# Loading a weight as two blocks of 8 partitions and one of 112 instead of one of 128

## The chip, the cores and the metric

The kernel runs on one core of a Trainium2 chip. The time is device microseconds of one execution. All numbers below are of undisturbed ("fast") runs. The span that the profile shows (187.6 us before) is about 1.3 us shorter than the timed figure of the same execution (188.87 us).

Weights and caches come from HBM into SBUF over 16 DMA engines. In the trace of the kernel before, the load of `w_gate` is 128 packets of 15360 B, one for each partition row, and 16 completions. From 20 to 180 us 16 packets are in flight for 90% of the time, and 15, 17 or 18 nearly all the rest, so each engine works at one packet after the other.

## The reference, cut to what matters

One decoding step of a transformer layer for two tokens: modulation, attention over a cache, then a gated feed-forward layer. The change touches only the load of `w_gate`, at the end:

```
h = layernorm(x) * (1 + cb) + sb                      # x: 2 x 640
x = x + gb * ((gelu(h @ w_gate) * (h @ w_up)) @ w_down)   # w_gate, w_up: 640 x 1536, w_down: 1536 x 640
```

Nearly all the work is reading: 76.88 MB in bf16.

## The kernel before

All loads go from one queue (SP), in the order in which they are needed: modulation weights, query weights, 16 K and 16 V blocks, three blocks of the output weight `wo`, then `w_gate`, two blocks of `w_up`, four of `w_down`. Every one of these loads fills all 128 partitions; blocks are cut by columns. The last loads, and the matmuls that wait for them:

```python
# each partition p holds rows 5p..5p+4 of w_gate: 5 x 1536 x 2 B = 15360 B, one packet
S.dma("sp", k_dma(wg_v.rearrange("p k n -> p (k n)"),
                  B_w_gate.rearrange("(p k) n -> p (k n)", k=KT)), sem_wg,
      writes=["wg"], deps=r3_dead, name="ld_wg")
# ... (w_up in WU_SPLIT = [(0,3),(3,2)], packets of 9216 and 6144 B;
#      w_down in WD_SPLIT = [(9,3),(0,5),(5,3),(8,1)], packets of 3840, 6400, 3840, 1280 B)
ffn_gu(0, wg_v, "gate", [(0, KT, "wg")])               # 20 matmuls, wait for ln2 and wg
# ... gelu
ffn_gu(1, wu_v, "up", [(k0, nk, ("wu", ci)) for ci, (k0, nk) in enumerate(WU_SPLIT)])
# ... geglu, transpose, then w_down block by block, two DVE operations, the store
```

Of the kernel before, what the change touches and what calls it, by code (L numbers as in the profile page):

```python
# [119 lines left out]
def bass_adaLN_cond__sliding_block_cached__geglu_ffn__decode_kernel(  # L120
# [20 lines left out]
    KT = D // P  # L141
# [28 lines left out]
    WQ_SPLIT = [(0, 2), (2, 3)]  # L170
    WO_SPLIT = [(0, 28), (28, 17), (45, 3)]
    NWQ, NWO = len(WQ_SPLIT), len(WO_SPLIT)
    WU_SPLIT = [(0, 3), (3, 2)]
    WD_SPLIT = [(9, 3), (0, 5), (5, 3), (8, 1)]
    RB = 16
# [11 lines left out]
    with es:  # L187
        S = _Sched(nc, es)
# [6 lines left out]
        wg_v = r3[:, 0:KT * F].rearrange("p (k n) -> p k n", k=KT)  # L195
        wu_v = r3[:, KT * F:2 * KT * F].rearrange("p (k n) -> p k n", k=KT)
# [56 lines left out]
        def bank(k):  # L253
            return ("bank", k)
# [1 line left out]
        sem_x = S.sem("d_x")  # L256
        sem_c = S.sem("d_c")
        sem_wm = S.sem("d_wm")
        sem_wg = S.sem("d_wg")
        sem_wu = [S.sem("d_wu%d" % i) for i in range(len(WU_SPLIT))]  # L260
        sem_wd = [S.sem("d_wd%d" % i) for i in range(len(WD_SPLIT))]
        sem_ring = [S.sem("d_ring%d" % i) for i in range(NS)]
# [2 lines left out]
        def k_dma(dst, src):  # L265
            return lambda e: e.dma_start(dst, src)  # L266
# [40 lines left out]
        def declare_ring(consumed=()):  # L307
            ring_state["done"].update(consumed)
            while ring_state["next"] < len(items):
                it = items[ring_state["next"]]  # L310
                if not all(h in ring_state["done"] for h in before_of[it]):
# [7 lines left out]
                       writes=["wm"], name="ld_wm")  # L319
# [4 lines left out]
        for nm, t in (("scT", scT), ("oT", oT), ("aT", aT)):  # L324
# [6 lines left out]
             reads=["ones_f"], writes=["ident_f"], name="ident_f")  # L331
        S.op("pool", lambda e: e.tensor_copy(out=ident_b[:, :], in_=ident_f[:, :]),
             reads=["ident_f"], writes=["ident_b"], name="ident_b")
# [3 lines left out]
             reads=["ones_b"], writes=["selrow"], name="selrow")  # L337
# [3 lines left out]
             reads=["ones_b"], writes=["selg"], name="selg")  # L341
        for b in range(B):
# [4 lines left out]
                 reads=["ones_b"], writes=[("selq", b)], name="selq%d" % b)  # L347
# [4 lines left out]
             reads=["ones_b"], writes=["ztmp"], name="ztmp")  # L352
# [6 lines left out]
             reads=["ones_f", "bcL"], writes=["bcL"], name="bcLh")  # L359
# [5 lines left out]
             reads=["bcR"], writes=["bcR"] + [("bcR", z) for z in range(2)], name="bcRd")  # L365
# [4 lines left out]
             reads=["ident_f"], writes=["mask_h"], name="mask_h")  # L370
        S.op("dve", lambda e: e.tensor_reduce(out=st32[:, :], in_=ident_f[:, :].rearrange("p (i m) -> p m i", m=32), axis=AX.X, op=ALU.add),
             reads=["ident_f"], writes=["st32"], name="st32")
# [3 lines left out]
             reads=["st32"], writes=["selstat"], name="selstat")  # L376
# [3 lines left out]
        def c_T(e):  # L380
            last = None
            for j in range(KT):
# [4 lines left out]
             reads=[bank(BK_T)], writes=["scT"], name="silu")  # L387
        S.op("dve", lambda e: e.tensor_copy(out=X[:, :], in_=xr[:, :]),
             reads=["xr"], writes=["X"], name="x_f32")
# [20 lines left out]
        def ln_mod(tag, opc_idx, s_idx, dst_bf):  # L410
# [7 lines left out]
            def f(e):  # L418
# [14 lines left out]
             reads=["mask_h"], writes=["maskc"], name="maskc")  # L433
        S.op("dve", lambda e: e.tensor_reduce(out=zsel[:, :, X0:X0 + P].rearrange("p q (h m) -> p q h m", m=32)[:, :, :, 0],
                                              in_=ztmp[:, :, :, :].rearrange("p i q h -> p q h i"), axis=AX.X, op=ALU.max),
             reads=["ztmp", "zsel"], writes=["zsel"], name="zsel")

        mod_pe = []
        for half in range(2):
            def f(e, half=half):  # L440
                last = None
                for k in range(KT):
# [9 lines left out]
                 reads=[bank(half)], writes=[("modR", half)], name="mod%d_evac" % half)  # L452
            S.op("dve", lambda e, half=half: e.tensor_scalar(out=opc[:, half, :], in0=modR[:, 3 * half + 1, :], scalar1=1.0, scalar2=None, op0=ALU.add),
                 reads=[("modR", half)], writes=[("opc", half)], name="opc%d" % half)
# [17 lines left out]
        for n in range(NQB):  # L472
            if n % 2 == 0:
                S.op("act", lambda e, n=n: e.activation(out=qrow[:, n * QW:(n + 1) * QW], in_=ps[:, n, :], func=ACTF.Copy),  # L474
                     reads=[bank(n)], writes=[("qrow", n)], name="q1_evac%d" % n)
            else:
                S.op("dve", lambda e, n=n: e.tensor_copy(out=qrow[:, n * QW:(n + 1) * QW], in_=ps[:, n, :]),  # L477
                     reads=[bank(n)], writes=[("qrow", n)], name="q1_evac%d" % n)
        for u, (n, b) in enumerate((n, b) for n in range(NQB) for b in range(B)):
            bk = BK_T + u % 4  # L480
            S.op("pe", lambda e, n=n, b=b, bk=bk: e.matmul(ps[:, bk, :], lhsT=selq[:, b, :], rhs=qrow[:, n * QW:(n + 1) * QW], start=True, stop=True),
                 reads=[("selq", b), ("qrow", n)], writes=[bank(bk)], name="q2_%d_%d" % (n, b))
            S.op("act", lambda e, n=n, b=b, bk=bk: e.activation(out=qbc[:, b, n * QW:(n + 1) * QW], in_=ps[:, bk, :], func=ACTF.Copy),  # L483
                 reads=[bank(bk)], writes=[("qbc", b, n)], name="q2_evac%d_%d" % (n, b))
# [98 lines left out]
        for g in range(NG + 2):  # L583
# [23 lines left out]
            if prev:  # L607
# [5 lines left out]
             reads=[bank(BK_OT)], writes=["oT"], name="oT")  # L613
        for ci, (t0, n) in enumerate(WO_SPLIT):
            def f(e, ci=ci, t0=t0, n=n):
# [11 lines left out]
        assert ring_state["next"] == len(items)  # L627

        r3_dead = [wm_dma] + mod_pe
        S.dma("sp", k_dma(wg_v.rearrange("p k n -> p (k n)"), B_w_gate.rearrange("(p k) n -> p (k n)", k=KT)), sem_wg,  # L630
              writes=["wg"], deps=r3_dead, name="ld_wg")
        for ci, (k0, nk) in enumerate(WU_SPLIT):
            S.dma("sp", k_dma(wu_v[:, k0:k0 + nk, :].rearrange("p k n -> p (k n)"), B_w_up.rearrange("(p k) n -> p (k n)", k=KT)[:, k0 * F:(k0 + nk) * F]), sem_wu[ci],
                  writes=[("wu", ci)], deps=r3_dead, name="ld_wu%d" % ci)
        wd_src = B_w_down.rearrange("(p r) n -> p (r n)", r=FC)
        for ci, (r0, nr) in enumerate(WD_SPLIT):
# [5 lines left out]
             reads=[bank(BK_M), ("modR", 0)], writes=["lnt"], name="ga_attn")  # L642
        S.op("dve", lambda e: e.tensor_tensor(out=X[:, :], in0=lnt[:, :], in1=X[:, :], op=ALU.add),
             reads=["lnt", "X"], writes=["X"], name="x1")
# [3 lines left out]
        def ffn_gu(bk, wv, name, splits):  # L648
            for ci, (k0, nk, key) in enumerate(splits):
                def f(e, k0=k0, nk=nk):  # L650
                    last = None
                    for k in range(k0, k0 + nk):
                        wk = wv[:, k, :].rearrange("p (m i r) -> p i m r", i=NR, r=FR)
                        for i in range(NR):
                            last = e.matmul(ps[32 * i:32 * i + B, bk, 0:FT].rearrange("p (m r) -> p m r", r=FR), lhsT=h2T[:, k, :],
                                            rhs=wk[:, i, :, :], start=(k == 0), stop=(k == KT - 1), tile_position=(0, 32 * i))
                    return last
                S.op("pe", f, reads=["ln2_out", key], writes=[bank(bk)], name="ffn_%s%d" % (name, ci))

        ffn_gu(0, wg_v, "gate", [(0, KT, "wg")])  # L660
        S.op("act", lambda e: e.activation(out=gl[:, :], in_=ps[:, 0, 0:FT], func=ACTF.Gelu_apprx_tanh),
             reads=[bank(0)], writes=["gl"], name="gelu")
        ffn_gu(1, wu_v, "up", [(k0, nk, ("wu", ci)) for ci, (k0, nk) in enumerate(WU_SPLIT)])
        S.op("dve", lambda e: e.tensor_tensor(out=aR[:, :], in0=ps[:, 1, 0:FT], in1=gl[:, :], op=ALU.mult),
             reads=[bank(1), "gl"], writes=["aR"], name="geglu")

        def a_T(e):
            last = None
            for i in range(NR):
# [7 lines left out]
             reads=[bank(2)], writes=["aT"], name="aT")  # L677
        for ci, (r0, nr) in enumerate(WD_SPLIT):
            def f(e, r0=r0, nr=nr):
# [10 lines left out]
             reads=[bank(BK_OT), ("modR", 1)], writes=["fin"], name="gb_y")  # L690
        S.op("dve", lambda e: e.tensor_tensor(out=finb[:, :], in0=fin[:, :], in1=X[:, :], op=ALU.add),
             reads=["fin", "X"], writes=["finb"], name="outR")
        S.dma("sp", k_dma(out[:, 0, :].rearrange("b (i n) -> i b n", i=NR), finb[0:P:RB, :]),
              sem_out, reads=["finb"], name="st_out")
# [35 lines left out]
```

## Time and profile before

| | before |
|---|---|
| time, median of 4 runs beside the change | 189.06 us (188.81 to 189.14) |
| HBM read | 76.88 MB, 410 GB/s over the span |
| load queue, share of 16 engines' span | 97.1% |
| `w_gate`: last completion | 175.37 us |
| `w_down`: last completion | 184.75 us |

These are lines of the page of the kernel before. The rows `DMA` and `GB/s` cut the span in 40 slices (a digit is tenths of busy DMA engines). The queue rows give packets, MB and the share of 16 engines' span. The last line is the chain that ended last.

```profile
span 187.6 us, 2409 instructions
...
DMA  7999998999999999999999999999999999999991
GB/s 254 402 451 435 430 459 372 422 435 424 430 422 422 427 425 426 427 424 420 419 432 432 422 423 422 421 438 422 424 423 422 419 488 428 416 384 442 398 396 45
...
q1 hardware_dynamic: 6492, 76.88, 97.1%
q8 instruction: 8, 0.13, 0.3%
...
DMA 71%; DVE 15%; PE 7%; ACT 2%; SPq 2%; issue 1%
```

DMA is full from the third slice on at about 425 GB/s. The chain of waits in order of time ends with this kernel's last load (start us, length us, what):

```profile
152.72 31.64 DMA r<-in_B_w_down_dram
184.41 0.72 PE ps L684 x16
185.16 0.34 DVE fin L689
185.52 0.32 DVE finb L691
```

The `w_down` loads were all issued long before; the last two blocks landed at 184.37 and 184.75 us (completion records), and after that come only the last matmuls, two DVE operations and the store. So the span of this kernel is the landing of its last load plus 3 us. The issue list (KB each, us from issue to landing) shows `w_gate` as one load:

```profile
r<-in_B_w_gate_dram SPq DMA_DIRECT2D x1, 1920.0 KB, 25.0
```

These are PE's matmuls on `w_gate`, on the first block of `w_up`, and on the last blocks of `w_down` (start us, busy us, ..., in brackets the idle time before and what ended it), from the timeline of the kernel before:

```profile
175.51 1.89 PE L655 MATMUL ps<-r,h2T 128*2 128x384 bf16 x20 [0.28 <-DVE h2T L427]
178.19 1.21 PE L655 MATMUL ps<-r,h2T 128*2 128x384 bf16 x12 [0.79 <-DMA r<-in_B_w_up_dram]
...
184.41 0.70 PE L684 MATMUL ps<-r,aT 128*17 128x160 bf16 x16 [0.62 <-DMA r<-in_B_w_down_dram]
```

The gate matmuls waited for the layer norm (DVE), not for `w_gate`, which had landed at 175.37. The later ones waited for DMA. And here is DMA in three stretches of 5 us, shortly before and while `w_gate` and `w_up` come in (last three columns: granted clock, DMA busy share, GB/s):

```profile
165.00:170.00 5.00, 2.40 (x88) 2.07 (x80) 0.00 (x0) 0.00 (x0) 0.00 (x0) 0.74 0.95 392
170.00:175.00 5.00, 1.69 (x86) 1.39 (x78) 2.33 (x9) 2.98 (x5) 0.00 (x0) 0.95 0.99 415
175.00:180.00 5.00, 3.34 (x52) 1.05 (x48) 0.17 (x1) 0.71 (x2) 0.00 (x0) 0.71 1.00 412
```

The trace holds each DMA packet with its start and duration, and each completion. Here a 15360 B packet takes 578 ns (median of 128; 573 to 591) and a 12288 B packet 464 ns (median): none of the 128 was visibly held up by another. But the engines do not stand level. The 16 completions of `w_gate` came at these times after the first of them:

```
0  0.04  0.05  0.08  0.15  0.16  0.28  0.52  0.81  0.98  1.53  1.55  1.61  1.67  1.69  1.92 us
```

The kernel ends with the latest engine. Part of the spread has a cause in this trace: the 8 packets of 16384 B of the instruction queue took 0.93 to 1.10 us each, between two packets of the load queue, and the data packet after one of them took 938 instead of 460 ns. By these figures (1.10 + 0.94 - 0.46) an engine falls about 1.6 us behind, an estimate; the same sum gives 1.5 to 1.6 us for each of the seven that began before 174 us. Six completions above are at least 1.53 us late; of the last `w_down` load, seven are over 1.4 us late.

### The profile page before, as it was taken

The page shows a single profiled execution, that of the slowest core. Times are in us where ns is not written, and L with a number is a line of the kernel's source. Part 1 is how long each engine was busy: PE and PEld are TensorE (multiplying, and loading weights), DVE is VectorE, ACT ScalarE, POOL GpSimd, SP SyncE. Part 2 cuts the span into 40 slices and gives each one's busy share as a digit, 9 for nine tenths or more (in the row PEclk, how much of TensorE's full clock was granted, in tenths as well). Part 3 has the DMA queues.
Part 4 walks back from the last instruction along what each step waited for, and adds up shares of the span by engine and source line. Part 5 has one row for each costly group of instructions (what it writes and reads, how often), then busy time and mean ns, then how long its engine had stood idle before and what let it go on. Part 6 is the DMA issues. An engine that isn't in the chain of part 4 may idle for free.

```text
span 187.6 us, 2409 instructions
## 1 busy us (share of the span) xinstructions
PE 107.5 (57%) x1039; PEld 51.1 (27%) x1039; DVE 98.2 (52%) x147; ACT 29.9 (16%) x72; POOL 5.1 (3%) x23
## 2 busy tenths in 40 slices
PE   0014730742968887676676655675497395364462
PEld 0011200210323443333423323233253152353121
DVE  6131100019588988886595695775865933003211
ACT  3041100082001221112011110210120103103400
POOL 8200000000000000000000000000000000000000
PEclk9999999997587999999879999999969967569696
DMA  7999998999999999999999999999999999999991
GB/s 254 402 451 435 430 459 372 422 435 424 430 422 422 427 425 426 427 424 420 419 432 432 422 423 422 421 438 422 424 423 422 419 488 428 416 384 442 398 396 45
DMA packets 6518, 77.03 MB, mean 411 GB/s; under 512 B 746, under 2 KB 876, under 8 KB 1516
## 3 DMA queue, kind: packets, MB, share of 16 engines
q1 hardware_dynamic: 6492, 76.88, 97.1%
q8 instruction: 8, 0.13, 0.3%
q10 hardware_dynamic: 16, 0.01, 0.0%
q14 instruction: 2, 0.02, 0.0%
HBM read 76.88 MB, written 0.00 MB: 410 GB/s over the span
## 4 chain that ended last, share of the span: by engine, by line
DMA 71%; DVE 15%; PE 7%; ACT 2%; SPq 2%; issue 1%
DMA ring<-in_A_k_cache_dram 37%; DMA ring<-in_A_wq_dram 17%; DMA r<-in_B_w_down_dram 17%; DVE prod L490 9%; PE ps L502 4%; DVE S_sb L509 4%; PE ps L467 2%; SPq L266 2%; ACT qbc L483 2%; DVE ps L485 1%; DVE M L512 1%; ACT qrow L474 1%; PE ps L526 0%; DVE bcR L519 0%; PE ps L684 0%
## 5 line engine op out<-in xcount | busy, mean ns | idle before, releaser
L490 DVE TENSOR_TENSOR prod<-ring,qbc 128x3072 bf16<-128x3072 bf16 x32 | 55.9, 1751 | 14.3 <-DMA ring<-in_A_k_cache_dram 14.3
L502 PE MATMUL ps<-prod,ident_b 128*128 128x512 bf16 x192 | 52.9, 419 | 14.4 <-DVE prod L490 14.4
L502 PEld LDWEIGHTS ps<-prod,ident_b 128*128 128x128 bf16 x192 | 17.5, 104 | 40.2 <-DVE prod L490 17.5
L509 DVE TENSOR_REDUCE S_sb<-ps 128x32 f32<-128x1024 f32 x16 | 19.3, 1206 | 2.1 <-PE ps L502 2.1
L526 PE MATMUL ps<-bcR,bcL 5*128 5x4 f32 x32 | 6.1, 258 | 21.9 <-DVE bcR L519 21.9
L563 ACT ACTIVATE On<-ps,rden 128x384 bf16<-128x384 f32 x16 | 9.3, 580 | 43.5 <-DVE rden L561 21.1
L551 PE MATMUL ps<-ring,E_sb 128*8 128x384 bf16 x256 | 15.5, 369 | 0.0
L534 ACT ACTIVATE E_sb<-Sb_sb 128x128 bf16<-128x128 f32 x16 | 5.0, 310 | 56.4 <-DVE Sb_sb L531 56.4
L467 PE MATMUL ps<-ring,hT 128*2 128x512 bf16 x60 | 6.7, 626 | 9.8 <-DMA ring<-in_A_wq_dram 8.8
L526 PEld LDWEIGHTS ps<-bcR,bcL 5*128 5x128 f32 x32 | 4.7, 183 | 26.1 <-DVE bcR L519 26.1
L477 DVE CAST qrow<-ps 128x512 bf16<-128x512 f32 x1 | 0.7, 692 | 15.7 <-PE ps L467 15.7
L622 PE MATMUL ps<-ring,oT 128*17 128x160 bf16 x192 | 5.5, 294 | 5.6 <-DMA ring<-in_A_wo_dram 5.6
L531 DVE TENSOR_TENSOR Sb_sb<-S_sb,ps 128x128 f32<-128x128 f32 x16 | 4.6, 287 | 7.6 <-PE ps L526 7.6
L540 PEld LDWEIGHTS ps<-denp,maskc 128*128 128x128 f32 x32 | 7.1, 224 | 3.7 <-ACT E_sb L534 0.9
L641 DVE TENSOR_TENSOR lnt<-ps,modR 128x160 f32<-128x160 f32 x1 | 0.3, 325 | 12.6 <-PE ps L622 12.6
L445 PE MATMUL ps<-r,scT 128*17 128x480 bf16 x40 | 4.3, 597 | 3.9 <-DMA r<-in_w_mod_dram 3.9
L622 PEld LDWEIGHTS ps<-ring,oT 128*17 128x17 bf16 x192 | 4.9, 117 | 6.2 <-DMA ring<-in_A_wo_dram 6.2
L551 PEld LDWEIGHTS ps<-ring,E_sb 128*8 128x8 bf16 x256 | 5.1, 90 | 3.7 <-issue 1.2
L396 PE MATMUL ps<-st,selstat 128*128 128x2 f32 x4 | 0.9, 298 | 8.6 <-ACT sqj L392 8.6
L467 PEld LDWEIGHTS ps<-ring,hT 128*2 128x2 bf16 x60 | 1.7, 114 | 14.7 <-DMA ring<-in_A_wq_dram 9.7
L576 PE MATMUL ps<-On,zsel 128*128 128x96 bf16 x64 | 5.2, 241 | 0.7 <-ACT On L563 0.7
L540 PE MATMUL ps<-denp,maskc 128*128 128x1 f32 x32 | 5.1, 230 | 0.8 <-ACT E_sb L534 0.8
(81 smaller groups left out, 71.2 us busy)
## 6 DMA issues: line engine op xcount, KB each, us to landing
ring<-in_A_k_cache_dram SPq DMA_DIRECT2D x16, 1536.0 KB, 24.4
ring<-in_A_v_cache_dram SPq DMA_DIRECT2D x16, 1536.0 KB, 24.2
r<-in_w_mod_dram SPq DMA_DIRECT2D x1, 4800.0 KB, 14.3
ring<-in_A_wq_dram SPq DMA_DIRECT2D x1, 4608.0 KB, 32.3
ring<-in_A_wo_dram SPq DMA_DIRECT2D x1, 4480.0 KB, 23.4
ring<-in_A_wq_dram SPq DMA_DIRECT2D x1, 3072.0 KB, 21.2
ring<-in_A_wo_dram SPq DMA_DIRECT2D x1, 2720.0 KB, 24.1
r<-in_B_w_gate_dram SPq DMA_DIRECT2D x1, 1920.0 KB, 25.0
```

Source lines behind the costliest of these rows:

```text
L467: last = e.matmul(ps[32 * i:32 * i + B, n, :], lhsT=hT[:, k, :], rhs=wv[:, kk, i, n * QW:(n + 1) * QW], start=(k == 0), stop=(k == KT - 1) ...
L490: S.op("dve", lambda e: e.tensor_tensor(out=prod[:, 2 * (g % 2) + ci, :, :], in0=ring[:, sl, ci * JC * Dh:(ci + 1) * JC * Dh].rearrange("p ...
L502: last = e.matmul(o_ap, lhsT=ident_b[:, :], rhs=prod[:, pz, :, t * GC:(t + 1) * GC], start=(t == 0), stop=(t == NCH - 1))
L509: S.op("dve", lambda e: e.tensor_reduce(out=S_sb[:, z, :], in_=ps[:, 2 * z:2 * z + 2, :].rearrange("p k (j c) -> p (k j) c", c=GC), axis=A ...
L526: S.op("pe", lambda e: e.matmul(ps[:, BK_T, P:P + HQ], lhsT=bcL[:, :], rhs=bcR[:, z, :], start=True, stop=True), reads=[("bcR", z), "bcL"] ...
L531: S.op("dve", lambda e: e.tensor_tensor(out=Sb_sb[:, z, :, :], in0=S_sb[:, z, :].unsqueeze(2).broadcast_to([P, J, HQ]), in1=ps[:, BK_T, P: ...
L534: S.op("act", lambda e: e.activation(out=E_sb[:, z, :, :], in_=Sb_sb[:, z, :, :], func=ACTF.Exp, scale=SCALE, accum_out=denp[:, z:z + 1]), ...
L540: S.op("pe", lambda e: e.matmul(ps[:, BK_T, P + 16:P + 17], lhsT=maskc[:, :], rhs=denp[:, z:z + 1], start=True, stop=True), reads=[("denp" ...
L551: last = e.matmul(ps[32 * i:32 * i + 2 * HQ, BK_O, 0:ON], lhsT=E_sb[:, z, 2 * jp:2 * jp + 2, :].rearrange("p j h -> p (j h)"), rhs=ring[:, ...
L563: S.op("act", lambda e: e.activation(out=On[:, quad % 2, b, :], in_=ps[:, BK_O, 0:ON], func=ACTF.Identity, scale=rden[:, z:z + 1]), reads= ...
L576: last = e.matmul(ps[:, BK_OT, 0:B * NT].rearrange("p (b t) -> p b t", b=B), lhsT=zsel[:, jj, x:x + P], rhs=On[:, quad % 2, :, jj * Dh + d ...
L622: last = e.matmul(ps[32 * i:32 * i + RM, BK_M, 0:DR], lhsT=oT[:, t, :], rhs=wv[:, tl, i, :], start=(t == 0), stop=(t == NT - 1), tile_posi ...
```

## The change

The intent is to give half of the engines less to do. An 8-row load is expected to run on 8 engines with one packet each, a 112-row load on 16 engines with 7 packets each. Then eight engines carry 2 + 7 = 9 packets of 15360 B and the other eight carry 7, where all had 8.

```diff
+    WG_SPLIT = [(112, 120), (120, 128), (0, 112)]
...
-        sem_wg = S.sem("d_wg")
+        sem_wg = [S.sem("d_wg%d" % i) for i in range(len(WG_SPLIT))]
...
-        S.dma("sp", k_dma(wg_v..., B_w_gate...), sem_wg, writes=["wg"], deps=r3_dead, name="ld_wg")
+        wg_d, wg_s = wg_v.rearrange("p k n -> p (k n)"), B_w_gate.rearrange("(p k) n -> p (k n)", k=KT)
+        for ci, (p0, p1) in enumerate(WG_SPLIT):
+            S.dma("sp", k_dma(wg_d[p0:p1, :], wg_s[p0:p1, :]), sem_wg[ci], writes=[("wg", ci)], deps=r3_dead, name="ld_wg%d" % ci)
...
-        ffn_gu(0, wg_v, "gate", [(0, KT, "wg")])
+        ffn_gu(0, wg_v, "gate", [(0, KT, [("wg", ci) for ci in range(len(WG_SPLIT))])])
```

(The first load line is shortened. The remaining edits only turn a key into a list of keys.)

More of the change, by code (lines that the diff above doesn't have):

```diff
@@ L629, in bass_adaLN_cond__sliding_block_cached__geglu_ffn__decode_kernel @@
         r3_dead = [wm_dma] + mod_pe
-        S.dma("sp", k_dma(wg_v.rearrange("p k n -> p (k n)"), B_w_gate.rearrange("(p k) n -> p (k n)", k=KT)), sem_wg,
-              writes=["wg"], deps=r3_dead, name="ld_wg")
+        wg_d, wg_s = wg_v.rearrange("p k n -> p (k n)"), B_w_gate.rearrange("(p k) n -> p (k n)", k=KT)
+        for ci, (p0, p1) in enumerate(WG_SPLIT):
+            S.dma("sp", k_dma(wg_d[p0:p1, :], wg_s[p0:p1, :]), sem_wg[ci], writes=[("wg", ci)], deps=r3_dead, name="ld_wg%d" % ci)
         for ci, (k0, nk) in enumerate(WU_SPLIT):
@@ L657, in f @@
                     return last
-                S.op("pe", f, reads=["ln2_out", key], writes=[bank(bk)], name="ffn_%s%d" % (name, ci))
-        ffn_gu(0, wg_v, "gate", [(0, KT, "wg")])
+                S.op("pe", f, reads=["ln2_out"] + key, writes=[bank(bk)], name="ffn_%s%d" % (name, ci))
+        ffn_gu(0, wg_v, "gate", [(0, KT, [("wg", ci) for ci in range(len(WG_SPLIT))])])
         S.op("act", lambda e: e.activation(out=gl[:, :], in_=ps[:, 0, 0:FT], func=ACTF.Gelu_apprx_tanh),
              reads=[bank(0)], writes=["gl"], name="gelu")
-        ffn_gu(1, wu_v, "up", [(k0, nk, ("wu", ci)) for ci, (k0, nk) in enumerate(WU_SPLIT)])
+        ffn_gu(1, wu_v, "up", [(k0, nk, [("wu", ci)]) for ci, (k0, nk) in enumerate(WU_SPLIT)])
         S.op("dve", lambda e: e.tensor_tensor(out=aR[:, :], in0=ps[:, 1, 0:FT], in1=gl[:, :], op=ALU.mult),
```

## The prediction

Passages are cut from the prediction where marked: they told how partitions, engines and transfer rates belong together, and which engines are hit. With them went one term of the sum, 3.1 us for the two 8-row blocks. With the 1 to 2 us for the 112-row block, the sum came to 4 to 5 us on top of 189 us; the figure was 193.0 us. "Engines 0-7" there and below are only names for the eight engines that run the 8-row loads: the trace numbers no engines.

> **What bounds the kernel now.** The DMA engines do. The page's slices show DMA at 0.9 or more from the third slice to the last but one; the queue table gives the load queue 97.1% of 16 engines' span (76.88 MB at 410 GB/s). The chain that ended last is 71% DMA, and its last link is w_down: 31.64 us from issue to 184.37, then 0.72 us of matmuls, 0.34 and 0.32 us on DVE and the store (span 187.6). So the time is the landing of the last w_down block plus about 3 us. All weight loads are queued by 162.5 us (timeline), so two more issues of 0.43 us each cost nothing.
>
> **How the 16 engines stand.** Read packet by packet, each engine runs its own queue back to back: 15,360 B takes 578 ns, 12,288 B 464 ns, alone on the engine. The 16 completions of each DMA are spread: for w_gate's they lie at 0 to 0.52 us (8 of them), 0.81, 0.98, and 1.53 to 1.92 us (6). Cause: the instruction queue's 16 KB packets (8 in the queue table), about 1.0 to 1.1 us each plus a slow packet after, each delays one engine by about 1.5 us, hitting seven engines before the end. [...] So probably the late half is engines 8 to 15.
>
> **Intent, costed.** [...] Engines 0-7 then carry 2+7=9 rows, 8-15 carry 7: plus and minus 578 ns. If only that counted, the last completion would be that of an early-half engine at 0.92+0.59=1.51 us instead of 1.83 us at the last block: gain 0.3 us, 188.7 us. Were the late engines in 0-7 it would cost 0.6 us.
>
> **What I expect to spoil it.** [...] The 112-row block, 7 rows per engine, [...] a small queue model adds 1 to 2 us. Nothing later rebalances, and w_down's landing moves by all of it: all on the critical path. Added besides: two hidden PE waits.
>
> **Prediction.** 193.0 us, range 188.6 to 195.5. Faster by over 2%: 0.01; within 2%: 0.46; slower by over 2%: 0.53.
>
> **What would show it.** Right: w_gate packets over 1 us (up to 2.3 us) in the 8-row blocks; w_gate landing, gate matmuls and the w_down landing some 3 to 5 us later; GB/s dip near 170 us; DMA share still full; tail after landing unchanged. Wrong: packets stay 578 ns, gate start at 175.5 us unmoved, w_down landing moves -0.3 or +0.6 us.
>
> **What would make it wrong.** [...] a row-to-engine map other than one row each; the 112-row block mapped more badly (rows dealt in turn), giving over +6 us.

## The result, and the profile after

The change made the kernel slower: 195.60 us (195.27 to 196.10, 4 runs) against 189.06 us, 6.5 us more. The ratio is 1.0351, with a 95% interval of 1.0325 to 1.0377. A ratio here is the mean time of one kernel's fast runs over that of the other's of the same rounds, so it is not quite the ratio of the two medians.

The page of the changed kernel:

```profile
span 194.5 us, 2411 instructions
...
DMA  7999989999999999999999999999999999999990
GB/s 253 411 423 435 485 375 419 427 425 427 430 425 427 425 421 425 427 425 425 425 427 425 430 418 429 422 430 427 420 430 453 435 420 416 346 225 221 339 373 22
...
q1 hardware_dynamic: 6508, 76.88, 96.9%
```

The `DMA` row still reads 9 nearly everywhere and the queue is still busy 96.9% of the span; what fell is `GB/s`, from about 425 to 346, 225, 221 and 339 in four slices near the end. A packet counts as busy time for as long as it is in flight, and here those of 15360 B took 1114 ns in the median instead of 578. By stretches of the changed kernel (same columns as above):

```profile
165.00:170.00 5.00, 1.93 (x60) 1.60 (x48) 0.00 (x0) 0.00 (x0) 0.00 (x0) 0.50 1.01 351
170.00:175.00 5.00, 3.03 (x80) 2.38 (x81) 0.97 (x3) 0.53 (x3) 0.00 (x0) 0.50 1.07 226
175.00:180.00 5.00, 0.93 (x22) 0.78 (x22) 1.53 (x7) 2.67 (x3) 0.00 (x0) 0.50 0.96 218
180.00:185.00 5.00, 1.90 (x20) 0.63 (x20) 0.00 (x0) 0.39 (x1) 0.00 (x0) 0.50 0.95 345
```

From 170 to 180 us the engines moved 226 and 218 GB/s, where the kernel before had 415 and 412, at a DMA share of 0.96 to 1.07 (a packet counts whole in the stretch in which it starts, hence above 1).

The issue list has the three loads; the 112-row block landed 31.5 us after its issue, where the whole weight took 25.0:

```profile
r<-in_B_w_gate_dram SPq DMA_DIRECT2D x1, 1680.0 KB, 31.5
...
r<-in_B_w_gate_dram SPq DMA_DIRECT2D x2, 120.0 KB
```

PE on the gate, the first `w_up` block and the last `w_down` blocks, timeline of the changed kernel:

```profile
182.66 1.90 PE L657 MATMUL ps<-r,h2T 128*2 128x384 bf16 x20 [4.88 <-DMA r<-in_B_w_gate_dram]
185.13 1.22 PE L657 MATMUL ps<-r,h2T 128*2 128x384 bf16 x12 [0.57 <-DMA r<-in_B_w_up_dram]
...
191.34 0.65 PE L686 MATMUL ps<-r,aT 128*17 128x160 bf16 x16 [0.64 <-DMA r<-in_B_w_down_dram]
```

The gate matmuls now start at 182.66 instead of 175.51 and wait for `w_gate`, whose last completion came at 182.53 us instead of 175.37. The rest follows at its old distance, as the chain shows:

```profile
153.24 38.05 DMA r<-in_B_w_down_dram
191.34 0.39 PE ps L686 x12
191.74 0.28 PE ps L686 x4
192.04 0.34 DVE fin L691
192.40 0.33 DVE finb L693
```

The last `w_down` block lands at 191.69 us (184.75 before), and the tail after it is as long as it was. The lower granted clock in some stretches (0.50) had no part in it: the 20 gate matmuls took 1.90 us, 1.89 before. So the whole loss arose while `w_gate` was coming in, and nothing gave it back.

Packet by packet: the 128 packets of 15360 B took 1114 ns in the median (607 to 1468), against 578 (573 to 591). This holds for both kinds of blocks: even the shortest of the 128 (607 ns) took longer than the longest before (591). The loads on either side suffered too: the packets of 9216 B (`w_up`, first block, loaded just as before) took 520 ns in the mean against 354, those of 3840 B (the last `wo` block and two blocks of `w_down`) 177 against 152. An average engine carries 8 packets of each of the first two sizes and 24 of 3840 B. Times the growth of the mean, this is 8 x 0.522 = 4.2 us in `w_gate`, 8 x 0.166 = 1.3 us in `w_up` and 24 x 0.025 = 0.6 us in the others: 6.1 us. The mean of the 16 completions of the last load moved by about as much in the trace, 6.2 us (183.78 to 189.94). The last of the 16 moved further, by 6.9 us (which is also by how much the traced span grew, 187.6 to 194.5), because the engines also drifted apart: from the first to the last completion it was 1.83 us before and is 3.28 us now.

The completions also tell how many engines an 8-row block uses. Each 8-row block left 9 semaphore events in the trace, one at issue and eight when data landed; the 112-row block left 16, and so did the whole `w_gate` before. That fits eight engines with one packet each.

### The profile page after: what moved, and what is told of

It reads as the page before. It is cut to its first block, busy times and chain, and to the rows that moved or that the text cites. A ratio compares the mean times of both kernels' runs of the same rounds, so it can differ in the third digit from the quotient of the medians.

```text
span 194.5 us, 2411 instructions
## 1 busy us (share of the span) xinstructions
PE 104.1 (53%) x1038; PEld 50.7 (26%) x1039; DVE 98.0 (50%) x147; ACT 29.9 (15%) x72; POOL 5.1 (3%) x23
## 3 DMA queue, kind: packets, MB, share of 16 engines
q1 hardware_dynamic: 6508, 76.88, 96.9%
## 4 chain that ended last, share of the span: by engine, by line
DMA 73%; DVE 16%; PE 5%; ACT 2%; SPq 2%; issue 1%
DMA ring<-in_A_k_cache_dram 36%; DMA r<-in_B_w_down_dram 20%; DMA ring<-in_A_wq_dram 17%; DVE prod L491 10%; DVE S_sb L510 4%; PE ps L503 2%; PE ps L468 2%; SPq L267 2%; ACT qbc L484 2%; DVE ps L486 1%; DVE M L513 1%; ACT qrow L475 1%; PE ps L527 0%; DVE bcR L520 0%; PE ps L686 0%
## 5 line engine op out<-in xcount | busy, mean ns | idle before, releaser
L503 PE MATMUL ps<-prod,ident_b 128*128 128x512 bf16 x192 | 49.0, 395 | 16.5 <-DVE prod L491 16.5
L503 PEld LDWEIGHTS ps<-prod,ident_b 128*128 128x128 bf16 x192 | 16.7, 100 | 39.3 <-DVE prod L491 20.4
L552 PE MATMUL ps<-ring,E_sb 128*8 128x384 bf16 x256 | 14.4, 350 | 0.0
L623 PE MATMUL ps<-ring,oT 128*17 128x160 bf16 x192 | 6.9, 337 | 7.6 <-DMA ring<-in_A_wo_dram 7.5
L623 PEld LDWEIGHTS ps<-ring,oT 128*17 128x17 bf16 x192 | 6.0, 133 | 8.5 <-DMA ring<-in_A_wo_dram 8.5
L541 PEld LDWEIGHTS ps<-denp,maskc 128*128 128x128 f32 x32 | 6.6, 208 | 3.5 <-ACT E_sb L535 0.9
L657 PE MATMUL ps<-r,h2T 128*2 128x384 bf16 x40 | 4.0, 485 | 6.1 <-DMA r<-in_B_w_gate_dram 4.9
L666 DVE TENSOR_TENSOR aR<-ps,gl 128x384 bf16<-128x384 f32 x1 | 0.6, 557 | 10.0 <-PE ps L657 10.0
## 6 DMA issues: line engine op xcount, KB each, us to landing
r<-in_B_w_gate_dram SPq DMA_DIRECT2D x1, 1680.0 KB, 31.5
```

The source lines that it names most:

```text
L503: last = e.matmul(o_ap, lhsT=ident_b[:, :], rhs=prod[:, pz, :, t * GC:(t + 1) * GC], start=(t == 0), stop=(t == NCH - 1))
L541: S.op("pe", lambda e: e.matmul(ps[:, BK_T, P + 16:P + 17], lhsT=maskc[:, :], rhs=denp[:, z:z + 1], start=True, stop=True), reads=[("denp" ...
L552: last = e.matmul(ps[32 * i:32 * i + 2 * HQ, BK_O, 0:ON], lhsT=E_sb[:, z, 2 * jp:2 * jp + 2, :].rearrange("p j h -> p (j h)"), rhs=ring[:, ...
L623: last = e.matmul(ps[32 * i:32 * i + RM, BK_M, 0:DR], lhsT=oT[:, t, :], rhs=wv[:, tl, i, :], start=(t == 0), stop=(t == NT - 1), tile_posi ...
```

## The experiments

Four explanations were to be told apart:

- Theory P (partitions): what counts is which SBUF partitions are written at the same time.
- Theory L (load): the uneven number of packets per engine, and nothing else.
- Theory N (number): each further DMA, or (N2) each DMA that has not 128 rows, costs a fixed time.
- Theory S (source): the reading side; blocks of rows read HBM unevenly.

The experiments ran in three groups (e1 to e4, e6 to e9, e10 and e11), each on a chip of its own with the kernel before beside it; "before" is 188.9 to 189.0 us in all three. Losses in us are differences of medians; the ratios are of means.

| run | time, us (median) | ratio to before, 95% interval |
|---|---|---|
| e1, only the 112-row block | 193.12 | 1.0218 (1.0188 to 1.0247) |
| e2, 16 + 112 | 195.12 | 1.0325 (1.0307 to 1.0343) |
| e3, three column blocks of 128 rows | 189.02 | 1.0009 (0.9992 to 1.0026) |
| e4, 64 + 64 | 195.06 | 1.0326 (1.0291 to 1.0360) |
| e6, 64 + 64, source rows strided | 195.52 | 1.0343 (1.0313 to 1.0372) |
| e7, full load + two extra blocks, 8 neighbouring partitions each | 191.71 | 1.0143 (1.0128 to 1.0159) |
| e8, the same blocks on every fourth partition from 0 to 60 | 189.43 | 1.0024 (1.0009 to 1.0039) |
| e9, the same blocks on every fourth partition from 64 to 124 | 191.41 | 1.0120 (1.0099 to 1.0141) |
| e10, one fifth of the columns split as in the change | 190.74 | 1.0092 (1.0078 to 1.0106) |
| e11, three fifths | 193.01 | 1.0216 (1.0198 to 1.0234) |

### e1_112_only: the large block by itself

```diff
-    WG_SPLIT = [(112, 120), (120, 128), (0, 112)]
+    WG_SPLIT = [(0, 112)]
```

> Only the 112-row block is loaded (rows 112-127 of the gate weights stay stale: wrong result on purpose); every engine carries 7 rows instead of 8. Theory P [...]: packets of the block take about 1.0 us instead of 0.58 and the kernel is 1.5 to 4 us slower than before although it moves 0.58 us less. Theory L (only the load per engine counts: one packet more on half of the engines): 0.4 to 0.6 us faster than before. Theory N (each further DMA in the queue costs, whatever its rows): one DMA, so no slower than before.

The result is wrong (16 rows keep old data). It was 4.2 us slower than before, a little more than the 1.5 to 4 us expected, although there were 112 packets instead of 128, one less for an engine on average, and the queue held no further DMA. That rules out theories L and N for this part. Stretches of e1:

```profile
170.00:175.00 5.00, 3.50 (x82) 2.87 (x82) 0.97 (x3) 1.05 (x3) 0.00 (x0) 0.50 1.05 252
175.00:180.00 5.00, 0.43 (x21) 0.28 (x20) 1.53 (x7) 2.15 (x3) 0.00 (x0) 0.50 0.93 252
```

Both stretches have 252 GB/s, against 415 and 412 before. The 112 packets took 1064 ns in the median. So about two thirds of the loss is in the block that was meant to be the harmless one.

### e2_16_112: meant to give every engine as many packets as before

```diff
+    WG_SPLIT = [(112, 128), (0, 112)]
```

> One block of 16 rows and one of 112: 1+7 = 8 packets on each of the 16 engines, as before. Theory L: the time of before, within 0.3 us (no engine has more). Theory P: [...] 3 to 5 us slower than before, nearly as slow as the change. Theory N: one DMA more, about a half of the loss of the change (two DMAs more), 3.3 us.

It was 6.2 us slower: almost the loss of the change, with a load that was meant to be even (how the 16 rows were dealt was not read from the trace). So the unevenness that gave the change its purpose is hardly what costs. The loss is above the 3 to 5 us that theory P had given.

### e3_cols3: three DMAs, cut by columns

```diff
+    WG_SPLIT = [(0, 2), (2, 4), (4, 5)]
-            S.dma("sp", k_dma(wg_d[p0:p1, :], wg_s[p0:p1, :]), ...
+            S.dma("sp", k_dma(wg_d[:, p0 * F:p1 * F], wg_s[:, p0 * F:p1 * F]), ...
```

> Three DMAs as in the change, but each has all 128 partitions and a part of the columns (packets of 6144, 6144 and 3072 bytes). Theory N: as slow as the change, 195.6 us. Theory P and theory L: the time of before, 189.0 us, within 0.3 us.

It ran as before (ratio 1.0009). The number of DMAs and of semaphores to wait for costs nothing here; theory N falls. Stretches of e3, to be held against those of e1 (416 GB/s in both):

```profile
170.00:175.00 5.00, 3.00 (x78) 2.61 (x66) 1.50 (x6) 1.71 (x3) 0.00 (x0) 0.50 1.03 416
175.00:180.00 5.00, 3.33 (x52) 1.44 (x52) 1.00 (x4) 1.98 (x3) 0.00 (x0) 0.62 1.01 416
```

### e4_halves and e6_src_stride2: destination or source

```diff
+    WG_SPLIT = [(0, 64), (64, 128)]                                   # e4 and e6
-            S.dma("sp", k_dma(wg_d[p0:p1, :], wg_s[p0:p1, :]), ...
+            S.dma("sp", k_dma(wg_d[p0:p1, :], wg_s[ci:P:2, :]), ...   # e6 alone; wrong result on purpose
```

> Two blocks of 64 rows, four packets on each engine and block, load even. Theory L: the time of before. Theory P: [...] 2.3 to 4.5 us slower than before [...]. Theory N: as e2.

> As e4_halves (two blocks of 64 neighbouring partitions as destination), but the source rows of each block are every second row of the weight (wrong result on purpose). Theory P [...]: as slow as e4_halves, 195.1 us, within 0.7 us. Theory S (the reading side: a block that covers a half of the tensor reads memory unevenly): clearly different from e4_halves, toward 189 us.

e4 was 6.2 us slower, more than the 2.3 to 4.5 expected. e6, which reads every second row, was as slow (6.5 us; the intervals of the two overlap). Reading other rows makes no difference that shows here; theory S falls. The stretch 175 to 180 us of e4:

```profile
175.00:180.00 5.00, 0.55 (x21) 0.38 (x21) 1.53 (x7) 2.27 (x3) 0.00 (x0) 0.50 0.98 215
```

and of e6:

```profile
175.00:180.00 5.00, 0.47 (x21) 0.30 (x21) 1.53 (x7) 2.39 (x3) 0.00 (x0) 0.66 0.96 205
```

215 and 205 GB/s are about half of the usual 425. They are not a measurement of the 64-row blocks alone: these stretches also hold packets of `w_up`, and from 170 to 175 us e4 moved 256 GB/s.

### e7, e8, e9: the same blocks, only the destination partitions differ

Here `w_gate` is loaded in one piece, as before. In front of it go two extra 8-row loads of 10240 B per row into a scratch tile that nobody uses (results are correct). Source rows, bytes and issue order are the same in all three; the partitions of the scratch tile are not. (That the same eight engines carry the extra blocks in all three is assumed; the trace numbers no engines.)

```diff
+        scr = sb("scr", [P, 5120], BF16)
+    WX = [slice(112, 120), slice(120, 128)]        # e7: 8 neighbouring partitions for each block
+    WX = [slice(0, 32, 4), slice(32, 64, 4)]       # e8: every fourth partition, 0 to 60
+    WX = [slice(64, 96, 4), slice(96, 128, 4)]     # e9: every fourth partition, 64 to 124
+        for ci, sl in enumerate(WX):
+            S.dma("sp", k_dma(scr[sl, :], wg_s[112 + 8 * ci:120 + 8 * ci, 0:5120]), sem_wg[ci], ...)
+        S.dma("sp", k_dma(wg_d, wg_s), sem_wg[2], ...)
```

> The gate weight in one 128-row load as before; in front of it two extra loads of 8 rows x 10240 B (the first 5120 columns of rows 112-127) into a scratch tile at partitions 112-119 and 120-127[...]. On engines 0-7 that is 2 x 0.39 us more load. Theory P: [...] 1.6 to 1.9 us slower than before. Theory L (load of the engine only; early engines have up to 0.9 us of slack): 0 to 0.3 us slower.

> As e7, same source rows, same bytes, but the scratch partitions are every fourth: 0,4,..28 and 32,36,..60[...]. Theory P: the time of before, 0 to 0.3 us slower. Theory L: the same as e7, whichever that is. This run also shows by its packet size which engines are 0 to 7.

> As e7 and e8, with scratch partitions 64,68,..92 and 96,100,..124[...]. Theory P: [...] 0.5 to 0.8 us slower than before, between e8 and e7. Theory L: the same as e7 and e8.

This is the decisive group. e7 was 2.7 us slower, e9 2.4 us, e8 0.4 us. By theory L they had to be equal. (All three lie above what theory P had given: 1.6 to 1.9, 0.5 to 0.8 and 0 to 0.3 us.) Packet durations, worked out from the trace's DMA records (medians, mean in brackets):

| | 10240 B packets (16) | 15360 B packets (128) |
|---|---|---|
| e8 (every fourth, 0 to 60) | 386 ns (388), 385 to 395 | 576 ns (577), 573 to 587 |
| e9 (every fourth, 64 to 124) | 607 ns (586), up to 753 | 578 ns (656), up to 1128 |
| e7 (112 to 119, 120 to 127) | 697 ns (669), up to 964 | 582 ns (729), up to 1349 |

In e8 not one of these packets was disturbed, the extra ones included. In e7 and e9 both the extra packets and those of the regular load slowed down, the longest to twice their length in e9 and to 2.5 times in e7. Why partitions 0 to 60 are harmless and 64 to 124 are not was not shown. The same shows in the stretches from 165 to 175 us. Those of e7:

```profile
165.00:170.00 5.00, 1.72 (x60) 1.51 (x52) 0.00 (x0) 0.00 (x0) 0.00 (x0) 0.84 1.01 343
170.00:175.00 5.00, 3.19 (x82) 2.81 (x82) 0.97 (x3) 0.94 (x3) 0.00 (x0) 0.69 0.99 319
```

Those of e8, where the rate stays at 402 and 421 GB/s although the extra blocks pass through:

```profile
165.00:170.00 5.00, 2.40 (x76) 2.07 (x72) 0.00 (x0) 0.00 (x0) 0.00 (x0) 0.50 0.97 402
170.00:175.00 5.00, 3.21 (x82) 2.82 (x74) 1.34 (x5) 1.56 (x3) 0.00 (x0) 0.50 1.01 421
```

And those of e9, where it falls to 341 and 379:

```profile
165.00:170.00 5.00, 2.35 (x76) 2.08 (x64) 0.00 (x0) 0.00 (x0) 0.00 (x0) 0.78 0.96 341
170.00:175.00 5.00, 2.85 (x81) 2.55 (x81) 0.97 (x3) 0.56 (x3) 0.00 (x0) 0.66 1.01 379
```

Which packets slowed shows something that the forecast for theory P does not contain. In it, the extra packets held up only a few of the others. At 171.03 us of e9 the trace has 16 packets in flight, and a single one of them is an extra packet (from 169.6 us on there are never more than two). But all 16 took 1.44 to 2.01 times as long as undisturbed packets of their size, and by 172 us all packets were back at the usual length. In the changed kernel each of the 235 data packets (those of 3840 B and more) that started from 169 to 181 us took at least 59% longer; in e8 not one of 175 from 168.5 to 173 us was even 10% longer. So the runs show that the destination partitions decide, and that the slowdown reaches all 16 packets in flight; how it gets there is open.

This fits the fact that e9 lost more than the 0.5 to 0.8 us expected. Its 3840 B packets were slow as well (mean 168 ns against 151 in e8). The extra packets and the added length of the others together make 1.6 us per engine on average, and by 1.6 us the mean of the 16 completions of the last load moved (183.78 to 185.39 us). The last completion moved 1.9 us, the rest being a wider spread. The traced execution was the fastest of e9's four (190.72 us), so 1.9 is to be compared with it and not with the 2.4 us of the median.

e8 tells one more thing. Only the eight engines of the 8-row loads carry 10240 B packets, so one can see when each of them got there. ("Engines 0 to 7" is only a name for these eight; the trace numbers no engines.) Start of each engine's first packet after the `wo` blocks, us after the earliest (engines 0 to 7 from their 10240 B packets; the other eight by following each engine's packets end to start):

```
engines 0 to 7 :  0     0.13  0.13  0.56  0.78  1.09  1.60  1.84
engines 8 to 15:  0.03  0.15  0.43  0.83  1.64  1.85  2.17  2.25
```

Late engines sit in both halves.

### e10 and e11: how the loss grows with the bytes

```diff
+    WG_SPLIT = [(0, P, 0, 4), (112, 120, 4, 5), (120, 128, 4, 5), (0, 112, 4, 5)]     # e10: rows, then fifths of the columns
+    WG_SPLIT = [(0, P, 0, 2), (112, 120, 2, 5), (120, 128, 2, 5), (0, 112, 2, 5)]     # e11
```

> The first four fifths of the columns in one 128-row load, only the last fifth (packets of 3072 B) split by rows as in the change: 8 + 8 + 112. Theory P (loss goes with the bytes [...]): 6.6 us / 5 = 1.3 us slower than before, 0.8 to 1.8. Theory N2 (each DMA that is not 128 rows costs a fixed time, whatever its bytes): about 6.6 us slower, as the change.

> Two fifths of the columns in one 128-row load, three fifths (packets of 9216 B) split by rows as in the change. Theory P: three fifths of 6.6 us, 3.3 to 4.6 us slower than before. Theory N2: about 6.6 us slower.

The loss was 1.8 us for one fifth of the bytes, 4.1 us for three fifths, 6.5 us for all (the change). That is about 1.2 us for each fifth and a rest of about 0.6 us. A fixed price for each DMA that has not 128 rows (theory N2) would have been the same in all three. The small rest was not examined.

No experiment gave a version that beats the kernel before. Whether one is possible was not shown. e3 (same time) and the kernel before remain the fastest.

## Why the prediction was wrong

It gave 193.0 us with a range of 188.6 to 195.5; measured were 195.60 us, just outside. It gave slower by over 2% a chance of 0.53, and that came true. Point by point:

- "The DMA engines do" bound the kernel, and w_down's landing "moves by all of it": right. The landing moved from 184.75 to 191.69 us, the tail stayed.
- Where the rows are written spoils the change: right, shown by e7 and e9 against e8 (same bytes and source; 2.7 and 2.4 us against 0.4), and e6 excludes the source rows (195.52 against 195.06 us in e4). That only the engines of the 8-row blocks pay for these blocks, as the sum assumed, was wrong: all 16 packets in flight at 171.03 us of e9 slowed, 1.44 to 2.01 times.
- The term that was mis-sized: the 112-row block, for which "a small queue model adds 1 to 2 us". Alone it cost 4.2 us (e1), with one packet per engine less to move; with that packet's 0.58 us added back it is about 4.8 us, an estimate. The model treated it as a small correction; it is the larger part. Longer packets of the block and of the loads before and after it, less the missing packet, account for 4.0 us per engine in e1. This is the step that failed. The prediction had itself named it among what would make it wrong ("the 112-row block mapped more badly", "over +6 us"); whether the cause is the order of the rows, as it says there, these runs do not tell.
- "Up to 2.3 us" for a packet of the 8-row blocks: too long. No 15360 B packet of the changed kernel took more than 1.47 us. The two blocks account for about 1.7 us (6.5 less the 4.8), not the 3.1 us that stood in the sum, so this error went the other way and hid part of the first. Why they cost less was not shown.
- "So probably the late half is engines 8 to 15": wrong. In e8, engines 0 to 7 hold three that are over 1 us late, engines 8 to 15 four. So the intent had probably nothing to win even if the destination cost nothing: taking e8's positions for those of the change, one packet more for an engine at 1.84 us gives 1.84 + 0.58 = 2.42 us, against 2.25 us for the latest one now. This estimate is 0.2 us slower, where the prediction hoped for 0.3 us faster. The 0.9 us (1.83 less 0.92) that it took off as slack of the early half was not there either.
- Two more issues and two more waits cost nothing: right (e3).
- What it said the profile would show: packets over 1 us, the dip in GB/s near 170 us, a full DMA share, an unchanged tail, all seen. "Some 3 to 5 us later" was 7.2 us for the gate matmuls and 6.9 us for the last landing.

What stays open: in which order the 112 rows are dealt to the engines, why some destination partitions cost time and others do not, and how this slows packets on all engines.

## What to carry to other kernels

Keep loads at 128 partitions and cut them by columns (e3 cost nothing, ratio 1.0009). Where a weight was loaded in blocks of fewer rows here, with DMA always busy (96.9% of the span), it cost roughly in proportion to the bytes (1.8, 4.1 and 6.5 us for one, three and five fifths) and slowed the loads before and after it (9216 B packets 520 ns instead of 354), on every engine. Before shifting work from "late" engines, find out which engines they are, and by a pair of runs like e8 and e9 whether the new destination costs time (189.43 against 191.41 us). A DMA row that stays at 9 hides such a stall (it read 9 here while GB/s fell from 425 to 221): read GB/s and the duration of a packet beside it.
